# Single vector steps, one-pass turning and longer sums in a kernel that mixes a Fourier layer with sliding-window attention

## The chip, the cores and the metric

The kernel runs on one core of a Trainium2 chip. The engines named below are TensorE (PE in the rows of the profile, with its weight loads as PEld), VectorE (DVE), ScalarE (ACT), GpSimd (POOL) and SyncE (SP), which only issues DMAs here. The metric is the time of one execution in microseconds of the device; the time of a kernel is the median of its runs.

## The reference

x is 2048x512, float32. Two branches and a gate, with 32 heads of 16 and a window of 256:

```python
g = _sigmoid((x * gate_w).sum(-1, keepdims=True))
# A: Fourier mixing with matrices, hidden axis, then sequence axis, real part
a = jnp.einsum("bsd,ed->bse", x, dft_hid_re)
b = jnp.einsum("bsd,ed->bse", x, dft_hid_im)
y = jnp.einsum("ts,bse->bte", dft_seq_re, a) - jnp.einsum("ts,bse->bte", dft_seq_im, b)
# B: causal attention in a sliding window, then the output projection
scores = jnp.einsum("bhqd,bhkd->bhqk", q, k) * (Dh ** -0.5)
mask = (idx[:, None] - idx[None, :] >= 0) & (idx[:, None] - idx[None, :] < W)
p = _softmax(jnp.where(mask[None, None], scores, -1e9), axis=-1)
o = jnp.einsum("bhqk,bhkd->bhqd", p, v)      # then @ wo
out = g * y + (1 - g) * o
```

## The kernel before

**Dense products.** A float32 matrix product is made of three products in float32r, a type that TensorE takes in one pass: each operand is split into `hi` (the operand rounded to float32r, a CAST) and `lo` (operand less `hi`, a TENSOR_TENSOR), and hi·hi, hi·lo and lo·hi are summed in PSUM (`TERMS`). Tiles `dqk`, `dv`, `dab` and `dc` are the PSUM targets of the projections of q and k, of v, of the hidden Fourier step and of the sequence Fourier step. All of it is one generator, `dense()`, which yields after each 128x512 product. The matrices of the sequence step come in 64 pieces of 128x1024 (`c_pieces`, `load_split`): DMA into `raw`, two CASTs and two TENSOR_TENSORs of 512 columns on DVE into `hi` and `lo`, then 24 products.

**Attention.** There are 4 groups of 8 heads (`NG`) and 32 blocks of 64 positions (`NB`), so N = 128 blocks, each with 4 pairs of heads (`NP`). The loop runs over n:

- `s_pair(n, p)` (S): one product of up to 128x320 scores into PSUM (`s`), then on DVE a masked minimum, which reads `s` and frees it (line 327), then on ACT an exponential that yields the row sum (line 330). Minimum and sum of each query land in a column of `ml`.
- `ml_rows(u)`, once per 8 blocks: turns `ml` (128x64) into rows with a product by the float32 identity `ident` on TensorE (line 337), the result in a PSUM tile of the `s` ring; DVE takes it apart into `mhl` and `lt`; DMAs write them to DRAM. `m_ring(u)` reads the minima back into rows 96 to 99 of `ring[0]`.
- `t_pair(k, p)` (T), `LAG` = 20 blocks behind S: the transposed scores with the minimum taken off by those rows, into PSUM (`t`); ACT's exponential writes them into `pt` (line 389); POOL zeroes the corners outside the window by affine selects (lines 394 and 398).
- `pv(n)`: sums of `pt` times v in float32 into `o`, the four pairs side by side on 32 columns each (line 415), for three blocks at a time. v is spread into `vpad` by POOL (`v_spread`). When 512 positions are done, DVE multiplies by the reciprocals of the sums (loaded from DRAM at that moment, line 422) and the result goes to `o_scr`.
- `make_pad`: DVE (3) and ACT (1) copy a block of q or k into the stationary tiles `pads`.

The tiles `s` and `t` share a ring of four PSUM banks (`ps_a`).

**Order.** TensorE's order is written out by hand: in each half of a pair `fill(n)` draws products from `dense()` at a rate of `FILL_FIRST`, `FILL_PROJ` or `FILL_SEQ` per two halves (12, 14 and 14.4 products per block). The orders of the other engines come from a scheduler, except that `behind(...)` and `late(...)` keep an instruction behind the last marked one of an engine. After the last sum the rest of `dense()` follows, with the output projection (`wo_block`, line 669) ahead of each of the last blocks of the sequence step; `attention_done` loads and splits `wo` into the place of `ring[0]`.

```python
            if p == 2 and k % 3 == 0:
                for j in range(k - 3, k):
                    if 0 <= j < N:
                        pv(j)
                if maxima < 16 and n > 8 * maxima + 8:
                    ml_rows(maxima)
```

Of the kernel before, what the change touches and what calls it, by code (L numbers as in the profile page):

```python
# [25 lines left out]
LAG = 20  # L26
WARM = 8
SWITCH = 4
FILL_FIRST, FILL_PROJ, FILL_SEQ = 3.0, 3.5, 3.6
# [3 lines left out]
def fnet_window_mix(ctx: ExitStack, tc: tile.TileContext, xT, x, wqk, wv, wr, wi, cr, ci, wo, gw, out):  # L33
# [69 lines left out]

    def load_split(src, act=False):
        return split_raw(load_raw(src), act)
# [51 lines left out]
    ident = const.tile([P, P], F32, name="ident")  # L157
    nc.gpsimd.memset(ident, 1.0)
    nc.gpsimd.affine_select(ident, ident, pattern=[[1, P]], compare_op=OP.is_equal, fill=0.0,
# [60 lines left out]

    def qk_evict(g, ss, i, ps):
        hl = ev.tile([P, 2, 512], F32R, name="hl", bufs=3)
        split_psum(hl[:, 0], hl[:, 1], ps, -SCALE if i == 0 else 1.0)
        ld(qk_scr[i][g][ss].rearrange("h x s -> x h s"), f(hl[:]))
# [12 lines left out]
    def qk_proj(g, ss, w):  # L237
        for i in range(2):
            ps = ps_d.tile([P, 512], F32, name="dqk", tag="d")
            n = 0  # L240
            for dk in range(DK):
                c = dk * 256 + i * 128
                for a, b in TERMS:
                    nc.tensor.matmul(ps, w[a][:, c:c + 128], XT[dk, ss][:, b],  # L244
                                     start=n == 0, stop=n == 11)
                    n += 1
                    if n < 12:
                        yield
# [11 lines left out]
    def row_proj(sb, w, ps):  # L260
        n = 0
        ss, c = divmod(sb, 4)
        for dk in range(DK):
            wh = [w[dk // 2][h][:, (dk % 2) * 512:(dk % 2) * 512 + 512] for h in range(2)]
            for a, b in TERMS:
                nc.tensor.matmul(ps, XT[dk, ss][:, a, c * 128:(c + 1) * 128], wh[b],  # L266
                                 start=n == 0, stop=n == 11)
                n += 1
                if n < 12:
# [15 lines left out]
    def ab_proj(i, sb, w, dst=None):  # L285
        ps = ps_d.tile([P, 512], F32, name="dab", tag="d")
        yield from row_proj(sb, w, ps)
        if dst is None:
            hl = ev.tile([P, 2, 512], F32R, name="hl", bufs=3)
# [23 lines left out]
    ML = {}  # L313

# [17 lines left out]

    def ml_rows(u):
        ml = ML.pop(u)
        nc.vector.reciprocal(ml[:, 1], ml[:, 1])
        pt = ps_a.tile([P, 512], F32, name="s", tag="st")
        nc.tensor.matmul(pt[:64, :P], ml.rearrange("p x c -> p (x c)"), ident, start=True, stop=True)  # L337
        hl = at.tile([32, 2, 2, 64], F32R, name="mhl", bufs=1)
        m = pt[:32, :P].rearrange("c (a r) -> c a r", a=2)
        nc.vector.tensor_scalar(hl[:, :, 0], m, -1.0, None, op0=OP.mult)  # L340
        nc.vector.scalar_tensor_tensor(hl[:, :, 1], m, -1.0, f(hl[:, :, 0]), op0=OP.mult, op1=OP.subtract)
        ld(m_scr[u].rearrange("x p (j r) -> (p j) x r", r=64), f(hl[:]).rearrange("c a h r -> c (a h) r"))
        lt = at.tile([64, P], F32, name="lt", bufs=1)
        nc.vector.tensor_copy(lt[32:64], pt[32:64, :P])
        for a in range(2):
            ls = l_scr[u]
            ld(bass.AP(tensor=ls.tensor, offset=ls.offset + a * 512, ap=[[1024, NP], [64, 8], [1, 64]]),
               lt[32:64, 64 * a:64 * a + 64])
# [8 lines left out]
    PT = {}  # L357

# [42 lines left out]
    def pv(n):  # L401
# [17 lines left out]
        if kb % 8 == 7:  # L419
            sb = kb // 8  # L420
            ps = OT.pop((g, sb))
            rl = ev.tile([P, 512], F32, name="ev")
            ls = l_scr[g * 4 + sb]
            ld(rl, bass.AP(tensor=ls.tensor, offset=ls.offset, ap=[[512, 2 * NP], [0, 16], [1, 512]]))
            nc.vector.tensor_mul(rl, ps, rl)
            ld(o_scr[sb][g], rl)


    def c_pieces(order):
        w, todo = {}, list(order)  # L430

        def get(k):
            for _ in range(2 if k not in w else 1):
                if todo:
                    cc, j = todo.pop(0)
                    w[cc, j] = load_split((cr, ci)[cc][j // 2, j % 2])
            return w.pop(k)
        return get
# [4 lines left out]
    def c_part(w, chunks, ab, ps, ends):  # L443
        for i in chunks:
            for a, b in TERMS:
                nc.tensor.matmul(ps, w[a][:, i % 8 * 128:i % 8 * 128 + 128], ab[SC[i]][:, b],  # L446
                                 start=i == ends[0] and a + b == 0, stop=i == ends[1] and a == 1)
                if i != chunks[-1] or a == 0:
# [37 lines left out]
    def dense():  # L486
# [7 lines left out]
        yield  # L494
        for ss in range(4):
            if ss:
                yield from qk_proj(0, ss, wq0)
            for c in range(4):
# [4 lines left out]
                if ss < 3:  # L503
                    if c in (1, 2):
                        late(split_x, ss + 1, (2 * c - 2, 2 * c - 1), ss == 0)
                        if ss < 2:
                            load_x(ss + 2, c - 1)
                elif c == 0:
                    raw = load_raw(wqk[1])
                    wraw = [load_raw(wi[0])]  # L510
                elif c == 2:
                    w = late(split_raw, raw)
        for g in range(1, NG):
            for ss in range(4):
                yield from qk_proj(g, ss, w)
                have.add(("qk", g, ss))
                if g == 1:
                    if ss == 0:
                        wraw.append(load_raw(wi[1]))
                    elif ss < 3:  # L520
                        if ss == 1:
                            ws = []
                        ws.append(late(split_raw, wraw[ss - 1]))
                        if ss == 1:
                            raw = load_raw(wqk[2])
                elif g == 2:
                    if ss == 0:
                        raw = load_raw(wqk[3])
                        wraw = [load_raw(wr[0])]
                    elif ss == 2:  # L530
                        nextw = late(split_raw, raw)
                        wraw.append(load_raw(wr[1]))
                elif ss in (0, 2):
                    if ss == 0:
                        ws = []
                    ws.append(late(split_raw, wraw[ss // 2]))
            if g == 1:
                for sb in range(16):
                    yield from ab_proj(1, sb, ws)
                    if sb == 1:  # L540
                        nextw = late(split_raw, raw)
            if g < 3:
                w = nextw
        ab = {}
        for sb in range(16):
# [3 lines left out]
            if sb < 10:  # L549
                if sb < 8:  # L550
                    gate_load(sb)
                if sb > 1:
                    late(gate, 2 * sb - 4)
                    late(gate, 2 * sb - 3)
# [7 lines left out]

# [235 lines left out]
```

## Time and profile before

| | |
|---|---|
| median of three runs | 869.66 us (869.17 to 870.4) |
| the profiled execution | 873.39 us |
| its span, first to last instruction | 871.3 us |
| mean granted TensorE clock | 0.998 |
| busy: PE, PEld, DVE, ACT, POOL | 860.5, 690.3, 611.3, 580.9, 384.6 us |
| HBM read and written | 106.69 and 50.07 MB |

PE's busy time counts each product from its start to its modelled end, so neighbours overlap: a 128x512 product lasts 395 ns in the rows, but the next one starts much sooner. What TensorE loses is therefore read from the distance between starts, and from the idle time of the weight loads (PEld) before an instruction, not from the busy share. S runs to 660 us of the span, T to 752 and the sums to 759, and after that only dense products and the output projection are left.

### The profile page before, as it was taken

The page shows a single profiled execution, that of the slowest core. Times are in us where ns is not written, and L with a number is a line of the kernel's source. Part 1 is how long each engine was busy: PE and PEld are TensorE (multiplying, and loading weights), DVE is VectorE, ACT ScalarE, POOL GpSimd, SP SyncE. Part 2 cuts the span into 40 slices and gives each one's busy share as a digit, 9 for nine tenths or more (in the row PEclk, how much of TensorE's full clock was granted, in tenths as well). Part 3 has the DMA queues.
Part 4 walks back from the last instruction along what each step waited for, and adds up shares of the span by engine and source line. Part 5 has one row for each costly group of instructions (what it writes and reads, how often), then busy time and mean ns, then how long its engine had stood idle before and what let it go on. Part 6 is the DMA issues. An engine that isn't in the chain of part 4 may idle for free.

```text
span 871.3 us, 17146 instructions
## 1 busy us (share of the span) xinstructions
PE 860.5 (99%) x5160; PEld 690.3 (79%) x5160; DVE 611.3 (70%) x1974; ACT 580.9 (67%) x1793; POOL 384.6 (44%) x1067
## 2 busy tenths in 40 slices
PE   8999999999999999999999999999999999999998
PEld 6888778787877778878788887878778787788886
DVE  4588987667878987878787777788876444564431
ACT  4388799888897987878788777877776454111110
POOL 9100054545444756656456566554546665200000
PEclk9999999999999999999999999999999999999999
DMA  6875796464749436644445354599944333485541
GB/s 229 266 226 155 248 262 197 153 214 158 241 158 289 130 105 225 172 130 135 134 131 170 105 163 133 156 349 256 329 148 159 123 118 114 130 263 192 189 145 48
DMA packets 93132, 157.87 MB, mean 181 GB/s; under 512 B 27120, under 2 KB 36080, under 8 KB 93040
## 3 DMA queue, kind: packets, MB, share of 16 engines
q1 hardware_dynamic: 92288, 155.61, 56.5%
q10 hardware_dynamic: 752, 1.18, 0.4%
q8 instruction: 40, 0.66, 0.3%
q14 instruction: 52, 0.43, 0.2%
HBM read 106.69 MB, written 50.07 MB: 180 GB/s over the span
## 4 chain that ended last, share of the span: by engine, by line
PE 92%; DVE 3%; DMA 2%; ACT 1%; issue 1%; SPq 0%; DVEq 0%; ACTq 0%
PE dc L446 40%; PE dab L266 9%; PE s L325 8%; PE o L415 8%; PE dqk L244 8%; PE t L388 8%; PE t L669 5%; PE dv L266 4%; DVE sm L327 1%; PE s L232 1%; DMA raw<-x 1%; ACT sm L330 1%; DMA ring<-qk_scr 1%; PE s L337 1%; DMA pt<-xT 0%
## 5 line engine op out<-in xcount | busy, mean ns | idle before, releaser
L446 PE MATMUL dc<-big,hi 128*128 128x512 f32 x1024 | 355.4, 395 | 0.0
L394 POOL TENSOR_SCALAR_AFFINE_SELECT pt<-pt 64x128 f32<-64x128 f32 x512 | 191.9, 375 | 276.4 <-ACT pt L389 261.2
L330 ACT ACTIVATE sm<-sm,ml 128x320 f32<-128x320 f32 (+4 forms) x512 | 277.3, 543 | 49.4 <-DVE ml L327 48.0
L327 DVE CUSTOM_DVE_ANT_0 sm<-s,mask 128x320 f32<-128x320 f32 (+4 forms) x512 | 230.7, 462 | 82.7 <-PE s L325 62.5
L389 ACT ACTIVATE pt<-t 128x320 f32<-128x320 f32 (+4 forms) x512 | 208.7, 412 | 89.8 <-PE t L388 86.2
L446 PEld LDWEIGHTS dc<-big,hi 128*128 128x128 f32 x1024 | 186.3, 188 | 32.6 <-issue 2.4
L446 PE MATMUL dc<-big,lo 128*128 128x512 f32 x512 | 201.6, 394 | 0.0
L398 POOL TENSOR_SCALAR_AFFINE_SELECT pt<-pt 64x128 f32<-64x128 f32 x448 | 161.9, 361 | 0.1
L325 PE MATMUL s<-ring,pad 128*128 128x320 f32 (+4 forms) x512 | 159.0, 310 | 0.9 <-DVE ml L327 0.5
L388 PE MATMUL t<-ring,pad 128*128 128x320 f32 (+4 forms) x512 | 155.1, 303 | 1.6 <-DVE ml L327 0.9
L310 DVE TENSOR_SCALAR pad<-ring,half 96x256 fp32r<-96x256 f32 x384 | 121.6, 358 | 24.2 <-PE t L388 22.0
L325 PEld LDWEIGHTS s<-ring,pad 128*128 128x128 f32 x512 | 96.0, 188 | 36.6 <-issue 7.4
L388 PEld LDWEIGHTS t<-ring,pad 128*128 128x128 f32 x512 | 96.1, 188 | 21.6 <-DVE ml L327 2.6
L446 PEld LDWEIGHTS dc<-big,lo 128*128 128x128 f32 x512 | 96.3, 188 | 10.6
L81 DVE TENSOR_TENSOR lo<-raw,hi 128x512 fp32r<-128x512 f32 x146 | 99.6, 712 | 1.4 <-PE dc L446 1.3
L330 ACT ACTIVATION_READ_ACCUMULATOR sm<-sm,ml 128x1 f32 x512 | 98.8, 193 | 0.0
L266 PE MATMUL dab<-hi,big 128*128 128x512 f32 x256 | 90.9, 396 | 0.0
L244 PE MATMUL dqk<-big,hi 128*128 128x512 f32 x240 | 86.7, 394 | 0.6 <-DVE hl L86 0.5
L80 DVE CAST hi<-raw 128x512 fp32r<-128x512 f32 x142 | 58.6, 453 | 38.3 <-PE dc L446 37.1
L415 PE MATMUL o<-pt,vpad 128*32 128x320 f32 (+4 forms) x1408 | 73.8, 351 | 0.0
L378 POOL COPY vpad<-vr 64x256 f32<-64x256 f32 x64 | 26.0, 405 | 91.1 <-DMA vr<-v_scr 72.0
L308 ACT ACTIVATE pad<-ring,half 96x256 fp32r<-96x256 f32 x128 | 64.1, 500 | 0.0
(82 smaller groups left out, 780.3 us busy)
## 6 DMA issues: line engine op xcount, KB each, us to landing
qk_scr<-hl SPq DMA_DIRECT2D x32, 512.0 KB
ring<-qk_scr SPq DMA_DIRECT2D x32, 512.0 KB
raw<-cr SPq DMA_DIRECT2D x32, 512.0 KB
raw<-ci SPq DMA_DIRECT2D x32, 512.0 KB
ab_scr<-hl SPq DMA_DIRECT2D x20, 512.0 KB
big<-ab_scr SPq DMA_DIRECT2D x20, 512.0 KB
r_scr<-ev SPq DMA_DIRECT2D x36, 256.0 KB
ev<-r_scr SPq DMA_DIRECT2D x36, 256.0 KB
```

What stands on the lines that cost most here:

```text
L244: nc.tensor.matmul(ps, w[a][:, c:c + 128], XT[dk, ss][:, b], start=n == 0, stop=n == 11)
L266: nc.tensor.matmul(ps, XT[dk, ss][:, a, c * 128:(c + 1) * 128], wh[b], start=n == 0, stop=n == 11)
L310: nc.vector.tensor_scalar(dst, src, half[:96, h:h + 1], None, op0=OP.mult)
L325: nc.tensor.matmul(ps[:, :w], PAD[0, n][:, p], ring[1][:, p, k0:k0 + w], start=True, stop=True)
L327: mark("dve", nc.vector.tensor_tensor_reduce(out=sm[:, :w], in0=ps[:, :w], in1=mask[:, WIN - w:], scale=1.0, scalar=3e38, op0=OP.add, op1= ...
L330: mark("act", nc.scalar.activation(sm[:, :w], sm[:, :w], AF.Exp, bias=nm[:, c], scale=-1.0, accum_out=l[:, c]))
L388: nc.tensor.matmul(ps[:, :w], PAD[1, n][:, p], ring[0][:, p, q0:q0 + w], start=True, stop=True)
L389: nc.scalar.activation(pt[:, p, :w], ps[:, :w], AF.Exp, scale=-1.0)
L394: nc.gpsimd.affine_select(a, a, pattern=[[0, 2], [1, 64]], compare_op=OP.is_ge, fill=0.0, base=0, channel_multiplier=-1)
L398: nc.gpsimd.affine_select(a, a, pattern=[[0, 2], [-1, 64]], compare_op=OP.is_gt, fill=0.0, base=0, channel_multiplier=1)
L415: nc.tensor.matmul(OT[g, sb][32 * p:32 * p + 32, q - sb * 512:e - sb * 512], v2[:, p], pt[:, p, q - q0:e - q0], start=first, stop=kb == 8 ...
L446: nc.tensor.matmul(ps, w[a][:, i % 8 * 128:i % 8 * 128 + 128], ab[SC[i]][:, b], start=i == ends[0] and a + b == 0, stop=i == ends[1] and a ...
```

## The change

- **Single steps.** `split_soon` puts the two CASTs and two TENSOR_TENSORs of a split into a list `jobs`; `job(n)` takes one from it at every sixth dense product (n % 6 == 3). The splits of x, of the projections' weights and of the pieces, and the products of the gate (`gate_soon`), go through it. Pieces are loaded two ahead instead of one (`Pieces`), and each `get` first empties the list.
- **One-pass turning.** `ident` becomes float32r. `ml_split` (at block 8u+8) takes the reciprocals and splits `ml` into float32r `hi` and `lo`; `ml_turn` (8u+9, third pair) makes two products; `ml_rows` (8u+9, fourth pair) takes the rows out, adding hi and lo of the sums; `m_ring` comes at 8u+11.
- **Sums.** `pv` runs for three blocks at a time as long as projections last, then for five. For that `pt` has six places: four as before, and two in `home`, which until then holds the pairs on their way to `qk_scr` and `ab_scr` (before: tiles `hl` of another pool, three of them). v is loaded and spread when its place is free. The reciprocals of the sums are loaded ahead (`l_load`) and the multiplication stands in `o_out`, a block's start later.
- **Numbers.** `LAG` 20 to 18, `FILL_PROJ` 3.5 to 4.0 and `FILL_SEQ` 3.6 to 3.7, so 12, 16 and 14.8 products per block. The float32 sums stand in 31 groups instead of 43 on TensorE, and 231 instead of 322 dense products are left at the last T, 63 of them instead of 92 between the last sum and the first output block; that one then has 5, 6 and 5 blocks of output rows at a time instead of 4, 4, 4 and 4.

```diff
-LAG = 20
+LAG = 18
-FILL_FIRST, FILL_PROJ, FILL_SEQ = 3.0, 3.5, 3.6
+FILL_FIRST, FILL_PROJ, FILL_SEQ = 3.0, 4.0, 3.7
...
+    jobs = []
+
+    def split_soon(raw):
+        hi = st.tile([P, 1024], F32R, name="hi")
+        lo = st.tile([P, 1024], F32R, name="lo")
+        for c in HALVES:
+            jobs.append(lambda c=c: late(nc.vector.tensor_copy, hi[:, c], raw[:, c]))
+            jobs.append(lambda c=c: late(nc.vector.tensor_sub, lo[:, c], raw[:, c], f(hi[:, c])))
+        return hi, lo
+
+    def job(n):
+        if n % 6 == 3 and jobs:
+            jobs.pop(0)()
...
+    def ml_split(u):
+        ml = ML.pop(u).rearrange("p x c -> p (x c)")
+        MH[u] = at.tile([P, 2, NP * 16], F32R, name="mlh", bufs=1)
+        with behind("dve"):
+            nc.vector.reciprocal(ml[:, 32:], ml[:, 32:])
+            nc.vector.tensor_copy(MH[u][:, 0], ml)
+            mark("dve", nc.vector.tensor_sub(MH[u][:, 1], ml, f(MH[u][:, 0])))
+
+    def ml_turn(u):
+        hl = MH.pop(u)
+        MT[u] = ps_a.tile([P, 512], F32, name="s", tag="st")
+        for h in range(2):
+            nc.tensor.matmul(MT[u][:64, h * P:h * P + P], hl[:, h], ident, start=True, stop=True)
+
     def ml_rows(u):
-        ml = ML.pop(u)
-        nc.vector.reciprocal(ml[:, 1], ml[:, 1])
-        pt = ps_a.tile([P, 512], F32, name="s", tag="st")
-        nc.tensor.matmul(pt[:64, :P], ml.rearrange("p x c -> p (x c)"), ident, start=True, stop=True)
...
+        with behind("dve"):
+            nc.vector.tensor_scalar(hl.rearrange("c a h r -> c h a r"), m, -1.0, None, op0=OP.mult)
+            nc.vector.tensor_copy(lt, pt[32:64, :P])
+            mark("dve", nc.vector.tensor_add(lt, pt[32:64, P:2 * P], lt))
...
-            PT[n] = at.tile([P, NP, WIN], F32, name="pt", bufs=4)
+            if "proj" in have:
+                more.append(n)
+            c = (n - more[0]) % 6 * NP * WIN if more else 3072
+            if c + NP * WIN <= 3072:
+                PT[n] = f(home[:, c:c + NP * WIN].rearrange("p (a b) -> p a b", a=NP))
+            else:
+                PT[n] = at.tile([P, NP, WIN], F32, name="pt", bufs=4)
...
+    TURN = (8, 1, ml_split), (9, 2, ml_turn), (9, 3, ml_rows), (11, 3, m_ring)
...
+            if p == 3 and k % 8 == 6 and 0 <= k < N:
+                l_load(k // 8)
+            if p == 0 and full:
+                o_out()
+            if p == 2 and (k - summed >= (5 if more else 3) or k == N):
+                for j in range(summed, k):
+                    pv(j)
+                summed = k
```

How this moves the instructions, at the places of which the prediction speaks. First VectorE in the sequence step, between the masked minima of S (`ISA sm`), before:

```order
L327 ISA sm,ml<-s,mask 128x320
L327 ISA ml 128x1
L80 CAST hi<-raw 128x512 x2
L327 ISA sm,ml<-s,mask 128x320
L327 ISA ml 128x1
L81 TENSOR_TENSOR lo<-raw,hi 128x512 x2
L327 ISA sm,ml<-s,mask 128x320
L327 ISA ml 128x1
L425 TENSOR_TENSOR ev<-o,ev 128x512
```

The same engine at the same stage, now:

```order
L352 ISA ml 128x1
L546 TENSOR_TENSOR lo<-raw,hi 128x512
L352 ISA sm,ml<-s,mask 128x320
L352 ISA ml 128x1
L546 CAST hi<-raw 128x512
L352 ISA sm,ml<-s,mask 128x320
L352 ISA ml 128x1
```

Between two minima stood two CASTs or two TENSOR_TENSORs, and now one of them. Next TensorE at a group of sums that has a turning of `ml` behind it, before (`o<-pt,vpad` are the sums, `s<-ident,ml` the turning in float32):

```order
L446 MATMUL dc<-big,hi 128x512
L415 MATMUL o<-pt,vpad_327 32x256 x4
L415 MATMUL o<-pt,vpad_327 32x192 x4
L415 MATMUL o<-pt,vpad_327 32x128 x4
L337 MATMUL s<-ident,ml 64x128
L325 MATMUL s<-ring_268,pad_1_264 128x320
```

TensorE now, a group of sums in the same stage:

```order
L512 MATMUL dc<-big,hi 128x512
L460 MATMUL o<-pt,vpad_326 32x320 x4
L460 MATMUL o<-home,vpad_326 32x320 x8
L460 MATMUL o<-pt,vpad_326 32x320 x4
L460 MATMUL o<-pt,vpad_327 32x256 x4
L350 MATMUL s<-ring_268,pad_1_264 128x320
```

And TensorE now at a turning:

```order
L433 MATMUL t<-ring_267,pad_1_266 128x320
L512 MATMUL dc<-big,hi 128x512
L370 MATMUL s<-ident,mlh 64x128 x2
L350 MATMUL s<-ring_268,pad_1_264 128x320
L512 MATMUL dc<-big,lo 128x512
```

A group holds five blocks instead of three, and the turning stands alone between dense products and S.

More of the change, by code (lines that the diff above doesn't have):

```diff
@@ L494, in dense, with x_job @@
         yield
+        def x_job(ss, dk):
+            late(split_x, ss, (dk,), ss == 1)
+            if dk % 2 and ss < 3:
+                load_x(ss + 1, dk // 2)
         for ss in range(4):
+            if ss < 3:
+                for dk in range(DK):
+                    jobs.append(lambda ss=ss, dk=dk: x_job(ss + 1, dk))
+                    jobs.append(lambda: None)
             if ss:
                 yield from qk_proj(0, ss, wq0)
+            if ss == 3:
+                w = split_soon(raw)
             for c in range(4):
@@ L548, in dense @@
             yield from ab_proj(0, sb, ws, ab.get(sb))
[L549 to L554, printed above, removed]
+            if sb in (1, 3):
+                gate_load(6 + sb // 2)
+            if sb < 7:
+                gate_soon(9 + sb)
+            if sb in (5, 7):
+                pieces.load()
+            if sb == 11:
+                pieces.split()
         for sc in range(4):
@@ L710, in fnet_window_mix, with v_next @@
     need(("v", 5))
-    for n in range(N + LAG + 2):
+    summed, spread, fresh = 0, 2, 0
+    def v_next(n):
+        if n < N:
+            for c in range(2):
+                need(("v", n % NB // 2 + c))
+            with behind(*(("sp",) if n < 8 else ())):
+                v_load(n)
+    for n in range(N + LAG + 1):
         if n in (1, 3, 5):
```

183 lines of the change are left out of this document (104 added, 79 removed).

## The prediction

> **What bounds the kernel now.** I read the page's busy line and chain first, then the waits, then the timeline at single places.
>
> ```profile
> PE 860.5 (99%) x5160; PEld 690.3 (79%) x5160; DVE 611.3 (70%) x1974; ACT 580.9 (67%) x1793; POOL 384.6 (44%) x1067
> ...
> PE 92%; DVE 3%; DMA 2%; ACT 1%; issue 1%; SPq 0%; DVEq 0%; ACTq 0%
> ```
>
> The chain in order of time has the price of a product where nothing disturbs it (start, us, what):
>
> ```profile
> 812.82 10.88 PE dc L446 x48
> ```
>
> That is 10.88/48 = 0.227 us for 128x512. TensorE holds 92% of the chain that ended last; every other engine has room on the whole. So the time is TensorE's stream of products, plus what it loses between them. A change that adds nothing to that stream can only gain what is lost, or lose more. The losses that other engines cause are in the waits (waiting line, releaser: total us, times, longest):
>
> ```profile
> DVE mhl L340 <- PE s L337: 24.8, 16, 2.7
> ...
> PEld s L325 <- ACT sm L330: 3.6, 7, 0.5
> ...
> PEld s L325 <- DVE ml L327: 3.3, 9, 0.6
> ...
> PEld t L388 <- DVE ml L327: 2.6, 6, 0.8
> ...
> PEld s L325 <- ACT pt L389: 2.0, 4, 0.8
> PEld o L415 <- POOL pt L398: 1.6, 5, 0.4
> PEld s L325 <- DVE ev L425: 1.6, 3, 0.5
> ...
> PEld t L388 <- ACT pt L389: 1.5, 4, 0.6
> ...
> PEld dqk L244 <- DVE hl L88: 1.0, 2, 0.5
> ...
> PEld dqk L244 <- DVE hl L86: 0.9, 1, 0.9
> ```
>
> VectorE releases 9 + 6 + 3 + 2 + 1 = 21 of these waits, 3.3 + 2.6 + 1.6 + 1.0 + 0.9 = 9.4 us of the weight loader. How much of such a wait the products lose, and where it comes from, one place shows:
>
> ```profile
> 610.83 0.67 DVE L81 TENSOR_TENSOR lo<-raw,hi 128x512 fp32r<-128x512 f32 x1
> ...
> 611.43 0.46 DVE L310 TENSOR_SCALAR pad<-ring,half 96x256 fp32r<-96x256 f32 x1
> ...
> 611.81 0.77 DVE L81 TENSOR_TENSOR lo<-raw,hi 128x512 fp32r<-128x512 f32 x1
> ...
> 612.40 0.39 PE L446 MATMUL dc<-big,hi 128*128 128x512 f32 x1
> 612.50 0.48 DVE L327 CUSTOM_DVE_ANT_0 sm<-s,mask 128x320 f32<-128x320 f32 x1
> ...
> 613.04 0.19 PEld L325 LDWEIGHTS s<-ring,pad 128*128 128x128 f32 x1 [0.60 <-DVE ml L327]
> 613.04 0.41 PE L325 MATMUL s<-ring,pad 128*128 128x320 f32 x1 [0.26 <-DVE ml L327]
> ```
>
> Two steps of a split and a pad stand on VectorE ahead of the minimum that empties a bank of S; the next S needs the bank. From start to start it is 613.04 - 612.40 = 0.64 us here, and 0.23 for such a product undisturbed, so 0.41 is lost where the loader idled 0.60: idle time less 0.19. The 21 waits on VectorE are thus worth 9.4 - 21 x 0.19 = 5.4 us, and the 15 on ScalarE's lines 330 and 389 worth 7.1 - 15 x 0.19 = 4.2 us.
>
> **The change part by part.** *Groups of sums.* A float32 group costs TensorE more than its columns, at both edges:
>
> ```profile
> 354.33 0.31 PE L388 MATMUL t<-ring,pad 128*128 128x320 f32 x1
> 354.47 0.39 PE L446 MATMUL dc<-big,hi 128*128 128x512 f32 x1
> 354.80 1.84 PE L415 MATMUL o<-pt,vpad 128*32 128x192 f32 x48
> 356.56 0.42 PE L325 MATMUL s<-ring,pad 128*128 128x320 f32 x1
> 356.82 0.40 PE L446 MATMUL dc<-big,hi 128*128 128x512 f32 x1
> ```
>
> The dense product ahead of it takes 354.80 - 354.47 = 0.33 us instead of 0.23, and the S behind it 356.82 - 356.56 = 0.26, where the T above takes 354.47 - 354.33 = 0.14. That is 0.22 us a group, and the order has 12 groups fewer (31, not 43): 12 x 0.22 = **2.6 us off**. What a group costs inside beside its columns (1.76 us for three blocks) these rows don't part; I count nothing for it, as the columns stay the same.
>
> *Turning.* Before, one float32 turning of two passes; now two products in one pass each.
>
> ```profile
> 332.82 0.19 PE L325 MATMUL s<-ring,pad 128*128 128x64 f32 x1
> 332.85 0.48 PE L446 MATMUL dc<-big,hi 128*128 128x512 f32 x1
> 333.16 0.31 PE L388 MATMUL t<-ring,pad 128*128 128x320 f32 x1
> ...
> 341.09 0.43 PE L337 MATMUL s<-ident,ml 128*64 128x128 f32 x2
> 341.45 0.33 PE L325 MATMUL s<-ring,pad 128*128 128x128 f32 x1
> ```
>
> The old one takes 341.45 - 341.09 = 0.36 us. The new form is not in the trace; its nearest row is a float32r product with few columns. S of 64 columns and the dense product after it take 333.16 - 332.82 = 0.34 together, 0.11 over the dense product alone: the columns are short, but the next weights come no sooner. At 0.06 each (128 columns at 0.23/512) the pair would cost 0.11, at 0.11 each 0.22. I take 0.20, near the row, as the second load has only the first short product to hide in: 16 x (0.36 - 0.20) = **2.6 us off**, with 2.2 and 4.0 as ends. By the Trainium skill's page "TensorE: Matmul & The Clock Gate", section "LDWEIGHTS (loading the stationary operand)", a load takes its columns over 1.2 GHz, an estimate of 53 ns for these 64 columns; by that the pair would cost about 0.11 us and this term be 4.0 us.
>
> *Single steps.* The numbers of splits and gate products stay; their places change.
>
> ```profile
> L310 DVE TENSOR_SCALAR pad<-ring,half 96x256 fp32r<-96x256 f32 x384 | 121.6, 358 | 24.2 <-PE t L388 22.0 <-DMA ring<-qk_scr 1.0 <-PE s L325 0.7
> L81 DVE TENSOR_TENSOR lo<-raw,hi 128x512 fp32r<-128x512 f32 x146 | 99.6, 712 | 1.4 <-PE dc L446 1.3
> ...
> L80 DVE CAST hi<-raw 128x512 fp32r<-128x512 f32 x142 | 58.6, 453 | 38.3 <-PE dc L446 37.1 <-DMA raw<-ci 1.0
> ...
> L344 DVE COPY lt<-s 32x128 f32<-32x128 f32 x16 | 4.5, 283 | 0.5
> ```
>
> Two TENSOR_TENSORs between two minima are 2 x 0.712 = 1.42 us, with the three pads 2.5; one of them with the pads is 1.79. I added these means up over VectorE's whole order: work of over 2 us between two minima stands at 31 places before and 11 now, and what exceeds 2 us falls from 17.5 to 2.9 us. The turning adds two small steps per 8 blocks (of some 0.3 us each, like L344), which VectorE's free 30% covers; and the multiplication by -1 for the rows no longer stands right behind a group of sums, where VectorE waited 24.8 us for the turning (first row of the waits). Waits don't vanish in proportion, as pads and evictions still fall together: I take two thirds of the 5.4, **3.6 us off**; the ends are 0 and 5.4.
>
> *Numbers.* More dense products per block (16 and 14.8, not 14 and 14.4) leave fewer for the end (231, not 322); their sum is the same, so TensorE's stream is the same length. Each pair of S and T gets up to 0.5 x 0.23 = 0.11 us longer, which gives ScalarE and VectorE more time per block. I count nothing for it; the 4.2 us of waits on ScalarE might shrink by half. `LAG` 18 starts T two blocks sooner and costs no product. If minima came back too late for T, T would wait, but they are read at block 8u+11 and first used at 8u+14. *Loads ahead* of pieces and reciprocals lift waits that TensorE does not feel (VectorE waits for a piece's DMA only 1.0 us in all, row L80): nothing.
>
> **The sum.** 2.6 + 2.6 + 3.6 = 8.8 us. The profiled execution took 873.39 us, its span 871.3 and 2.1 around it, so it would take 864.6. The median of the runs shown, 869.66, lies 3.7 below the profiled execution; I take the gain off there: 869.66 - 8.8 = **860.9 us**.
>
> **The rivals.** *The first output block comes too early (R1).* The order leaves 63 dense products, not 92, between the last sum and the first output block.
>
> ```profile
> 758.30 0.54 PE L415 MATMUL o<-pt,vpad 128*32 128x128 f32 x16
> ...
> 769.21 0.62 ACT L78 CAST os<-ev 128x512 fp32r<-128x512 f32 x1 [16.80 <-DMA ev<-o_scr]
> 769.86 0.69 DVE L81 TENSOR_TENSOR os<-ev,os 128x512 fp32r<-128x512 f32 x1 [3.85 <-ACT os L78]
> ```
>
> From the end of the last sum (758.84) to its first block split (770.55) it took 11.7 us, through VectorE, two DMAs and ScalarE. The cover is now 63 x 10.88/48 = 14.3 us. It holds by 2.6; SP's queue has a piece's load ahead of that read, which waits for the split of `wo`'s second half. If that puts 3 to 6 us on the way, TensorE waits up to 3.4: 864.3. Chance 0.14.
>
> *The waits stay (R2).* Steps now fall between nearly all minima; if each wait avoided is paid for at another place, the edges and turnings alone remain: 869.66 - 5.2 = 864.5, and with as many new waits on the turning's bank, held by VectorE's third step, as are saved (5.2), 869.7, no change. Chance 0.10.
>
> *Slower: selects held up by splits (R3).*
>
> ```profile
> 610.45 1.30 POOL L394 TENSOR_SCALAR_AFFINE_SELECT pt<-pt 64x128 f32<-64x128 f32 x1
> ...
> 612.69 0.29 POOL L398 TENSOR_SCALAR_AFFINE_SELECT pt<-pt 64x128 f32<-64x128 f32 x1
> ```
>
> A select that meets VectorE's split (610.83, above) shows 1.30 us, one that meets none 0.29: 1.0 more. With a split step in nearly every pair, the last select ahead of a group of sums meets one more often; were each of the 18 groups of five blocks held up for that 1.0 us, TensorE would lose 18 us: 860.9 + 18 = 879. It decides when POOL ends a block's selects over half a block after its T. Against it: POOL is busy 44% of the span, the group waits until the third pair of the next block, and the sums waited for line 398 five times for 1.6 us. The Trainium skill has the rule on the page "SBUF — State Buffer", section "SBUF: two separate sides": VectorE's steps with two SBUF inputs and GpSimd share a pair of ports as an exclusive lock, and whoever starts second is blocked for the whole instruction; the 1.30 agrees. Chance 0.07.
>
> *All waits go (R4)*, on VectorE (5.4) and half on ScalarE (2.1), and the turning is cheap (4.0): 869.66 - 14.1 = 855.6. Chance 0.12.
>
> **How the numbers follow.** My forecast has 0.57, R1 0.14, R2 0.10, R3 0.07, R4 0.12. The range 855.5 to 868 holds the forecast with its terms' ends, R1, R4 and half of R2. A difference of 0.2%, 1.7 us, is about what a measurement of this kernel can tell from none: faster is all but R3 and part of R2, 0.86; same 0.06; slower 0.08.
>
> **What would show it.** In the new profile: 31 groups with the same 0.22 at the edges; two turning products at 0.2 us a pair; under 2 us of waits of PEld on lines of the minima; TensorE's first output product without idle time ahead of it. A wait of PEld on POOL of over 5 us would be R3, idle time ahead of the output projection R1. If the span falls by less than 4 us with all of that as forecast, losses between products that no wait shows have grown, and the account is wrong.

## The result and the profile after

The kernel after takes 870.33 us (median of 14 runs, 867.32 to 874.2), the kernel before beside it 870.31 us (14 runs, 869.17 to 874.53): ratio 0.9996, 95% interval 0.9981 to 1.0012. No change can be measured; the forecast was 860.9, with 855.5 to 868.0 as its range. The profiled execution of after took 868.91 us, its span 867.2.

Busy line and chain of the page of after:

```profile
PE 853.2 (98%) x5160; PEld 693.5 (80%) x5160; DVE 616.4 (71%) x2006; ACT 588.4 (68%) x1793; POOL 371.6 (43%) x1067
...
PE 94%; DMA 3%; DVE 1%; issue 0%; ACT 0%; ACTq 0%; POOL 0%; SPq 0%; DVEq 0%
```

TensorE is busy 7.3 us less than before (860.5), which is the direction that fewer group edges and a cheaper turning give, and yet the chain has DMAs for 3% (2% before), and 14.0 us of the span are idle on TensorE (10.8 before): it stands still more. The waits say where (waiting line, releaser: total us, times, longest):

```profile
PE s L350 <- ACT pt L434: 7.6, 2, 4.1
...
ACT pt L434 <- DMA big<-ab_scr: 4.8, 1, 4.8
ACT pt L434 <- DMA l_scr<-mhl: 4.3, 1, 4.3
PEld s L350 <- DVE ml L352: 3.6, 10, 0.6
...
DVE mhl L379 <- PE s L370: 2.6, 1, 2.6
```

VectorE's wait for the turning, 24.8 us before, is down to 2.6. The longest wait on a minimum is still 0.6. New are two long waits on ScalarE's exponential of T (line 434): 7.6 us of TensorE in two pauses, each of which ended when ScalarE had waited for a DMA. Stage by stage (window: us, busy time of the engines with counts, granted clock, DMA share, GB/s), before:

```profile
550.00:575.00 25.00, 25.00 (x186) 19.72 (x185) 17.79 (x63) 18.81 (x60) 13.25 (x38) 1.00 0.80 250
575.00:600.00 25.00, 24.80 (x137) 19.27 (x137) 22.58 (x80) 19.76 (x69) 10.22 (x28) 1.00 0.91 301
600.00:625.00 25.00, 24.74 (x158) 19.74 (x157) 21.20 (x69) 19.98 (x63) 14.02 (x40) 1.00 1.04 333
```

and after:

```profile
550.00:575.00 25.00, 22.92 (x155) 17.76 (x153) 19.74 (x68) 16.08 (x51) 11.76 (x37) 1.00 1.01 271
575.00:600.00 25.00, 22.88 (x149) 18.54 (x150) 17.23 (x56) 16.86 (x56) 10.07 (x26) 0.93 0.78 258
600.00:625.00 25.00, 21.39 (x138) 17.14 (x137) 19.61 (x69) 16.16 (x54) 10.01 (x27) 1.00 1.00 284
```

This is the stretch in which the sixteen 512 KB tiles of the second half of the sequence step are loaded (`next_b`, `big<-ab_scr`). In both kernels the DMA share reaches 1.0 there; only after stands still. The first pause in the timeline of after:

```profile
559.92 0.38 SPq L56 DMA_DIRECT2D big<-ab_scr  x1
...
561.40 0.52 SPq L56 DMA_DIRECT2D ring<-qk_scr  x1
564.05 0.32 SPq L56 DMA_DIRECT2D m_scr<-mhl  x1
564.48 0.57 SPq L56 DMA_DIRECT2D ring<-qk_scr  x1
565.10 0.58 SPq L56 DMA_DIRECT2D big<-ab_scr  x1
...
571.68 0.19 ACT L355 ACTIVATION_READ_ACCUMULATOR sm<-sm,ml 128x1 f32 x1
...
575.88 0.64 ACTq L391 DMA_DIRECT2D ring<-m_scr  x1
576.63 0.44 ACT L434 ACTIVATE pt<-t 128x320 f32<-128x320 f32 x1 [4.75 <-DMA big<-ab_scr]
...
577.12 0.42 PE L350 MATMUL s<-ring,pad 128*128 128x320 f32 x1 [4.07 <-ACT pt L434]
```

ScalarE is done at 571.87 and then stands at `m_ring`, the DMA that brings the rows of minima back from DRAM, which it issues at 575.88 only. Behind `m_ring` in its queue are the exponentials that empty the PSUM banks, so TensorE stops. `m_ring` waits for two things: for the store `m_scr<-mhl` (issued 564.05), and for its own DMA semaphore. The program gives its hardware DMAs eight semaphores in turn, and a DMA is issued when the transfer that had its semaphore before has landed; here that is a `big` load issued after the store, and it landed at 575.80. In order of time the chain shows that load from issue to landing (start, us), and for the second pause a store of sums in the same part:

```profile
565.10 10.70 DMA big<-ab_scr
...
613.61 9.15 DMA l_scr<-mhl
```

The landings by the trace's semaphore updates: the two stores of minima took 10.0 and 10.1 us (564.05 to 574.05, 610.03 to 620.16); before, the stores in that stretch took 5.7 and 3.8. Of ScalarE's 4.0 and 3.6 us at `m_ring`, the stores account for 2.2 and 0.9, the semaphores for 1.8 and 2.6.

After the pause there is a second price (windows as above):

```profile
577.00:578.00 1.00, 0.88 (x3) 0.78 (x4) 0.43 (x3) 1.00 (x5) 0.00 (x0) 0.79 0.99 375
578.00:580.00 2.00, 2.00 (x7) 1.66 (x6) 1.32 (x6) 1.34 (x5) 1.55 (x4) 0.50 0.81 249
580.00:582.00 2.00, 2.00 (x10) 1.68 (x9) 1.85 (x7) 1.38 (x4) 1.08 (x4) 0.75 0.88 327
```

The granted clock is 0.50 for 3.4 us, and a dense product takes 0.43 us from start to start instead of 0.23. Counted that way, the two pauses cost 4.2 and 3.7 us and the slow products behind them about 1.7 each, some 11 us in all (the expectation of the first run counts 10.5). A run below that has neither pause is 8.8 us faster than this kernel.

### The profile page after: what moved, and what is told of

It is laid out like the page before. It is cut to its first block, busy times and chain, and to the rows that moved or that the text cites. A ratio compares the mean times of both kernels' runs of the same rounds, so it can differ in the third digit from the quotient of the medians.

```text
span 867.2 us, 17211 instructions
## 1 busy us (share of the span) xinstructions
PE 853.2 (98%) x5160; PEld 693.5 (80%) x5160; DVE 616.4 (71%) x2006; ACT 588.4 (68%) x1793; POOL 371.6 (43%) x1067
## 4 chain that ended last, share of the span: by engine, by line
PE 94%; DMA 3%; DVE 1%; issue 0%; ACT 0%; ACTq 0%; POOL 0%; SPq 0%; DVEq 0%
PE dc L512 39%; PE dab L288 10%; PE dqk L265 9%; PE s L350 9%; PE o L460 8%; PE t L433 8%; PE dv L288 5%; PE t L754 5%; DMA big<-ab_scr 1%; DMA vr<-v_scr 1%; DMA l_scr<-mhl 1%; PE s L253 1%; PE dv L551 0%; DVE pad L333 0%; DVE sm L352 0%
## 5 line engine op out<-in xcount | busy, mean ns | idle before, releaser
L352 DVE CUSTOM_DVE_ANT_0 sm<-s,mask 128x320 f32<-128x320 f32 (+4 forms) x512 | 235.5, 464 | 117.7 <-PE s L350 91.5
L439 POOL TENSOR_SCALAR_AFFINE_SELECT pt<-pt 64x128 f32<-64x128 f32 x392 | 139.5, 356 | 228.5 <-ACT pt L434 217.3
L434 ACT ACTIVATE pt<-t 128x320 f32<-128x320 f32 (+4 forms) x392 | 160.5, 411 | 59.2 <-PE t L433 48.0
L433 PE MATMUL t<-ring,pad 128*128 128x320 f32 (+4 forms) x512 | 155.1, 303 | 0.1
L333 DVE TENSOR_SCALAR pad<-ring,half 96x256 fp32r<-96x256 f32 x384 | 119.3, 358 | 19.0 <-PE t L433 18.6
L350 PEld LDWEIGHTS s<-ring,pad 128*128 128x128 f32 x512 | 96.5, 188 | 42.3 <-ACT pt L434 10.5
L443 POOL TENSOR_SCALAR_AFFINE_SELECT pt<-pt 64x128 f32<-64x128 f32 x344 | 117.4, 341 | 0.0
L433 PEld LDWEIGHTS t<-ring,pad 128*128 128x128 f32 x512 | 96.7, 189 | 21.7 <-DVE ml L352 0.9
L546 DVE TENSOR_TENSOR lo<-raw,hi 128x512 fp32r<-128x512 f32 x142 | 97.7, 698 | 0.0
L288 PE MATMUL dab<-hi,big 128*128 128x512 f32 x256 | 89.1, 393 | 0.0
L265 PE MATMUL dqk<-big,hi 128*128 128x512 f32 x240 | 84.9, 393 | 0.0
L439 POOL TENSOR_SCALAR_AFFINE_SELECT home<-home 64x128 f32<-64x128 f32 x120 | 48.1, 401 | 61.2 <-ACT home L434 53.3
L546 DVE CAST hi<-raw 128x512 fp32r<-128x512 f32 x142 | 61.3, 443 | 16.2 <-PE dc L512 15.8
```

What stands on the lines that cost most here:

```text
L265: nc.tensor.matmul(ps, w[a][:, c:c + 128], XT[dk, ss][:, b], start=n == 0, stop=n == 11)
L333: nc.vector.tensor_scalar(dst, src, half[:96, h:h + 1], None, op0=OP.mult)
L350: nc.tensor.matmul(ps[:, :w], PAD[0, n][:, p], ring[1][:, p, k0:k0 + w], start=True, stop=True)
L352: mark("dve", nc.vector.tensor_tensor_reduce(out=sm[:, :w], in0=ps[:, :w], in1=mask[:, WIN - w:], scale=1.0, scalar=3e38, op0=OP.add, op1= ...
L433: nc.tensor.matmul(ps[:, :w], PAD[1, n][:, p], ring[0][:, p, q0:q0 + w], start=True, stop=True)
L434: nc.scalar.activation(pt[:, p, :w], ps[:, :w], AF.Exp, scale=-1.0)
```

## The experiments

**The theory (A):** ScalarE, in order, stands at `m_ring` while the DMAs are slow, and that eats the gain. **Rivals:** the rows are too late for T anyway (B); the gain was never there (C); only the semaphore's former user holds `m_ring`, not the store (D). The differences below are between medians. The kernel before, taken again beside each group of runs, stood at 870.05 to 870.86 us, and by the ratios to it some of these differences come out up to 1 us smaller. First, `m_ring` one block later in the order:

```diff
-    TURN = (8, 1, ml_split), (9, 2, ml_turn), (9, 3, ml_rows), (11, 3, m_ring)
+    TURN = (8, 1, ml_split), (9, 2, ml_turn), (9, 3, ml_rows), (12, 3, m_ring)
```

> The kernel after, with the transfer of the minima's rows to the ring (m_ring, issued by ScalarE) one block later: (12, 3) for (11, 3). Theory A (ScalarE stands in its queue at m_ring until the rows' store has landed, twice for about 4 us, and TensorE with it): both pauses of TensorE (4.2 and 3.7 us) and the slow products behind them go, 870.3 - 10.5 = 859.8 us (858 to 862), and no wait on ACT pt over 1.5 us is left. Rival B (the rows simply come too late while the DMAs are busy): T waits for the rows instead, twice 3 to 6 us on DMA ring, 868 to 873. Rival C (the pauses are not what eats the gain): they go, and the time stays above 866.

Measured 864.42 us (863.15 to 865.17), 0.9937 of before (0.9925 to 0.9949). One number in the order gives 5.9 us. The longest wait on ACT pt is 0.5, no T waits for its rows (against B), and the time fell below 866 (against C). It is not 859.8, because one dense product now waits for a `big` load in the same stretch:

```profile
PEld dc L512 <- DMA big<-ab_scr: 2.2, 1, 2.2
PEld s L350 <- ACT pt L434: 2.0, 4, 0.5
PE dc L512 <- DMA big<-ab_scr: 1.8, 1, 1.8
```

The other way round, `m_ring` three quarters of a block earlier, where by the program's waits it stands, in the first of the two places, for its store alone:

```diff
-    TURN = (8, 1, ml_split), (9, 2, ml_turn), (9, 3, ml_rows), (11, 3, m_ring)
+    TURN = (8, 1, ml_split), (9, 2, ml_turn), (9, 3, ml_rows), (11, 0, m_ring)
```

> The kernel after with m_ring three quarters of a block earlier, (11, 0) for (11, 3): ScalarE reaches it 4.4 us earlier. In the trace of after, by the semaphores, the two stores landed at 574.05 and 620.16, 2.2 and 0.9 us after ScalarE stood at m_ring, and the transfers that had m_ring's semaphore before it landed 1.75 and 2.6 us later still. At (11, 0) m_ring of block 12 waits for its store alone. Theory A (the store's landing): ScalarE stands there 6.6 and 5.3 us, TensorE loses as much more as ScalarE, 870.3 + 4.3 = 874.6 us (872 to 877). Rival D (the semaphore's former user alone holds m_ring): the pauses of blocks 12 and 13 go, about 860 to 863.

Measured 872.54 us (867.86 to 875.51), 1.0023 of before (1.0004 to 1.0041; after's own interval, 0.9981 to 1.0012, touches it). The chain has the store from issue to landing, the waits have ScalarE behind it:

```profile
565.09 10.06 DMA m_scr<-mhl
...
ACT pt L434 <- DMA m_scr<-mhl: 12.6, 2, 6.4
...
PE t L433 <- ACT pt L434: 5.2, 1, 5.2
PE s L350 <- ACT pt L434: 5.1, 1, 5.1
```

D falls: with no foreign semaphore in the way the pause is longer. ScalarE stood 5.7 and 5.5 us at `m_ring` (6.6 and 5.3 expected), TensorE 2.7 us more in the two pauses than in after, and the time rose by 2.2, not by 4.3.

Why does the store take 10 us? It was put on ScalarE's own DMA queue:

```diff
-        ld(m_scr[u].rearrange("x p (j r) -> (p j) x r", r=64), f(hl).rearrange("c a h r -> c (a h) r"))
+        MH[u] = hl
...
+    def m_store(u):
+        with behind("act"):
+            nc.scalar.dma_start(m_scr[u].rearrange("x p (j r) -> (p j) x r", r=64),
+                                f(MH.pop(u)).rearrange("c a h r -> c (a h) r"))
...
-    TURN = (8, 1, ml_split), (9, 2, ml_turn), (9, 3, ml_rows), (11, 3, m_ring)
+    TURN = (8, 1, ml_split), (9, 2, ml_turn), (9, 3, ml_rows), (10, 2, m_store), (11, 3, m_ring)
```

> The kernel after, with the store of the minima's rows to DRAM issued by ScalarE's queue (at (10, 2)) and not by SyncE's; m_ring stays at (11, 3). If the store is late because it stands behind the large loads in SyncE's DMA queue (queue theory), it now lands in under 7 us in the same stretch, ScalarE doesn't wait, and the time is 859 to 862. If it is late because all 16 DMA engines are busy, whichever queue it comes from (saturation theory), it takes over 10 us again, both pauses stay at 3 us or more, and the time is 867 to 872.

Measured 867.69 us (865.13 to 874.48), ratio 0.9985 (0.9968 to 1.0002). The trace is of the execution that took 874.48. By the semaphore updates the two stores took 8.6 and 7.9 us, less than 10 but far from the 1.5 to 5.6 us of this run's other stores, and both pauses stayed, at 3.3 and 2.8 us. That lies between the two expectations, nearer to the second:

```profile
580.40 0.44 ACT L439 ACTIVATE pt<-t 128x320 f32<-128x320 f32 x1 [4.09 <-DMA l_scr<-mhl]
580.89 0.63 PE L350 MATMUL s<-ring,pad 128*128 128x320 f32 x1 [3.32 <-ACT pt L439]
```

So the store is slow from another queue too. The Trainium skill gives a reason on the page "DMA: Bandwidth & Descriptors", section "Issuing engines are not separate DMA queues": DMAs from any engine run on the same 16 DMA engines and interleave there. The 8.6 and 7.9 us agree. The run does not show that another queue could never help: its stores were issued 5.6 us ahead of the moment at which ScalarE was ready for `m_ring`, in after 7.8 and 9.2.

What stands ahead of the store in after are loads of the ring (issued 561.40 above). `LAG` sets their place:

```diff
-LAG = 18
+LAG = 20
```

> The kernel after with LAG 20 for 18: loads of the ring are issued two blocks later, so that they stand behind the store of the minima's rows in SyncE's queue, not right ahead of it. Queue theory: the store lands in under 9 us, both pauses go, 859 to 863. If the sixteen 512 KB loads of the second half alone delay the store (theory of the switch), the pauses stay: 867 to 872.

Measured 866.49 us (865.09 to 874.0), ratio 0.997 (0.9953 to 0.9987). The trace is of the slowest execution, 874.0, so its pauses are larger than the median's. The SyncE rows now have the store ahead of the ring:

```profile
561.45 0.38 SPq L56 DMA_DIRECT2D m_scr<-mhl  x1
...
566.09 1.28 SPq L56 DMA_DIRECT2D ring<-qk_scr  x2
```

and the two stores landed in 3.9 and 2.8 us. That part of the theory holds: with `LAG` 18 the ring's loads stand ahead of these two stores, and that makes them late. But the time is not 859 to 863. `m_ring` waited 2.0 us for a ring load that had its semaphore, and VectorE met the same queue at another place, the addition of r:

```profile
617.55 14.72 DMA ev<-r_scr
...
DVE ev L663 <- DMA ev<-r_scr: 6.5, 1, 6.5
PE t L433 <- DVE ml L352: 5.2, 1, 5.2
```

A load that took 14.7 us held VectorE for 6.5 and TensorE for 5.2. With `LAG` 20 and `m_ring` two blocks later as well:

```diff
-LAG = 18
+LAG = 20
...
-    TURN = (8, 1, ml_split), (9, 2, ml_turn), (9, 3, ml_rows), (11, 3, m_ring)
+    TURN = (8, 1, ml_split), (9, 2, ml_turn), (9, 3, ml_rows), (13, 3, m_ring)
```

> The kernel after with LAG 20 and m_ring at (13, 3), as far ahead of its first T as before: the loads of the ring stand behind the stores, and ScalarE reaches m_ring two blocks later than in the LAG 20 run. If m_ring was the only place at which the queues of that stretch stop TensorE: no pause over 1.5 us, 861 to 863. If the stretch's delays of 10 to 15 us stop another engine that waits in order (in the LAG 20 run VectorE stood 6.5 us at the addition of r, and TensorE 5.4): one such pause stays, 864 to 868.

Measured 865.78 us, ratio 0.9947 (0.9927 to 0.9966): ScalarE never waits at `m_ring`, and the pause at VectorE's addition stays, at 3.6 us by the waits (`PE t L433 <- DVE ml L352`). The second expectation it is. The rates alone:

```diff
-FILL_FIRST, FILL_PROJ, FILL_SEQ = 3.0, 4.0, 3.7
+FILL_FIRST, FILL_PROJ, FILL_SEQ = 3.0, 3.5, 3.6
```

> The kernel after with the old rates (FILL_PROJ 3.5, FILL_SEQ 3.6): the sixteen loads of the second half move by about a block against the blocks of S, the loads of the ring stay right ahead of the store. Queue theory: at least one store still has loads of the ring and of the second half ahead of it, so at least one pause of 3 us or more stays: 864 to 870. If it was only the chance meeting of the two (coincidence theory), both pauses go: 859 to 863.

Measured 866.04 us (864.14 to 868.29), ratio 0.9959 (0.9945 to 0.9973): one store (583.17) took 11.6 us, ScalarE stood 2.3 us, one pause of 2.3 us stayed, less than the 3 expected, and the other was gone, since the first store now lies ahead of the heavy stretch (it landed in 1.5 us).

Then the loads of the second half, spread over twice as many half blocks:

```diff
-SWITCH = 4
+SWITCH = 8
...
-            if after:
+            if after and c == 0:
```

> The kernel after with m_ring where it is, but the sixteen 512 KB loads of the second half spread over twice as many half blocks (SWITCH 8, one load a half block, not SWITCH 4 and two). If the DMA engines' load in that stretch makes the store of the rows late (saturation theory, which the store on ScalarE's own queue spoke for), the DMA share falls from 1.05 to about 0.85, both pauses of TensorE fall under 1 us each, and the time is 860 to 864. Rival: the loads of the ring ahead of the store do it; then the pauses stay at 3 us or more, and the time is 867 to 872.

Measured **861.51 us** (858.66 to 863.68), 0.9906 of before (0.989 to 0.9921), the fastest of all and faster than both kernels. No pause is over 0.9 us (windows of this run):

```profile
550.00:575.00 25.00, 24.86 (x166) 19.83 (x165) 21.46 (x73) 18.96 (x62) 13.16 (x40) 1.00 0.95 272
...
600.00:625.00 25.00, 24.40 (x152) 19.78 (x151) 22.23 (x74) 19.82 (x64) 13.99 (x39) 1.00 0.94 278
```

The time is as expected, the reason less so: the DMA share fell to 0.95 over 25 us, not to 0.85, and the stores still took 8.8 and 10.0 us. They landed just before ScalarE needed them (571.84 for 572.02, 613.35 for 613.82), and no semaphore held `m_ring` there for more than 0.6. That is a narrow escape, not a cure. `SWITCH` 8 also sends eight more blocks of the sequence step through DRAM half done (45 stores of `r_scr`, not 37), so the spread is not all that it changes. With `m_ring` later as well:

> Both: m_ring one block later and the loads of the second half spread (SWITCH 8). The wait of 2.0 us of a dense product for such a load (and some 0.5 us of slow products behind it), which m_ring later alone left, goes as well: 864.4 - 2.5 = 861.9 us (861 to 864). If the load in that stretch cost nothing beyond the two pauses: 864.4, no change against m_ring later alone.

Measured 862.72 us (861.74 to 863.93), ratio 0.9912 (0.9898 to 0.9925): no pause over 1.1 us in that stretch. The wait for a `big` load is gone; against the run above there is no difference to be measured. The control, `SWITCH` 8 in the kernel before:

> Control: the kernel before, with the loads of the second half spread (SWITCH 8, one a half block). Before has no pause of TensorE over 1 us in that stretch; what it lost there above its other stages is about 1.7 us. If the spread helped the kernel after only by keeping ScalarE from being held at m_ring, before gains little: 868.5 to 870.5. If spreading is a gain of its own: 861 to 864, as the kernel after got from it.

Measured 870.01 us, ratio 0.9992 (0.9979 to 1.0006): spreading those loads is worth nothing where no engine is caught. What it took from after was the pauses.

**The sizes of the terms,** on the kernel with `m_ring` one block later (864.42). The steps again in bursts:

```diff
-        if n % 6 == 3 and jobs:
+        while n % 24 == 3 and jobs:
             jobs.pop(0)()
```

> m_ring one block later, and VectorE's splits and gate products again in bursts (all queued steps of a piece after its third product, not one after every sixth). It sizes the term of the single steps by itself, against 864.4. The prediction's term: 3.6 us slower, 868.0. By what the products lost to VectorE in the two traces (3.9 us before, 2.6 with m_ring later): 1.3 slower, 865.7. No use at all: 864.4.

Measured 869.35 us, ratio 0.9987 (0.9979 to 0.9996): 4.9 us slower (4.4 by the ratios). The waits:

```profile
PEld t L433 <- DVE ml L352: 3.4, 9, 0.9
PEld s L370 <- DVE mlh L364: 3.0, 2, 1.7
```

A new one is among them: the turning of after needs a split by VectorE ahead of it, and bursts hold that up at two places. From the first product of a pair to the next product, the 16 turnings take 5.5 us here and 2.5 without bursts. So about 3.0 of the 4.9 us are a cost that bursts would have only with the new turning. Groups of three throughout:

```diff
-            if p == 2 and (k - summed >= (5 if more else 3) or k == N):
+            if p == 2 and (k - summed >= 3 or k == N):
```

> m_ring one block later, and groups of sums of three blocks throughout, not five late. It sizes the term of the groups, against 864.4. The prediction's term: 12 groups more by 0.22 us, 2.6 slower, 867.0. By the traces (all groups and the product ahead of them took 75.1 us before and 72.1 with m_ring later): 3.0 slower, 867.4. If longer groups hold up S and T as much as they save: 864.4.

Measured 868.71 us, ratio 0.9977 (0.9968 to 0.9986): 4.3 slower (3.5 by the ratios). Added up over the two traces, less what the products ahead cost undisturbed, the 43 groups with the products ahead of them take 75.1 us and the 31 take 72.4; the products behind them lose 1.3 us more. In this trace the one long wait for a `big` load is also longer, 3.0 us and with slow products behind it. The old turning, with `ident` and `ml` in float32:

```diff
-        for h in range(2):
-            nc.tensor.matmul(MT[u][:64, h * P:h * P + P], hl[:, h], ident, start=True, stop=True)
+        nc.tensor.matmul(MT[u][:64, :P], ml, ident, start=True, stop=True)
```

> m_ring one block later, and the old turning: one float32 product of two passes on the unsplit minima and sums, placed as in after. It sizes the term of the turning, against 864.4. The prediction's term: 16 x 0.16 = 2.6 us slower, 867.0. By the traces (the turning took 0.36 us before and 0.154 a pair with m_ring later): 3.3 slower, 867.7. If the turning's time is hidden in the waits around it: 864.4.

Measured 864.64 us, ratio 0.9938 (0.9919 to 0.9958): 0.2 slower, with some 2 us of uncertainty from the two intervals. On TensorE the old form does cost what it cost before, 0.36 us; the profiled span is 1.5 us longer (863.2 and 861.7). The term is smaller than its price on TensorE. The waits show a part of the rest: with `m_ring` one block later the weight loader waits 13 times, 5.4 us, for VectorE's minima ahead of S and T, and 12 of these waits stand within 7 us behind a turning; with the old form it waits there 4 times, 2.5 us, one of them behind a turning, and 6 times, 2.1 us, ahead of the turning itself. So the new turning costs waits behind it that the old one does not. Whether the bank that it keeps or VectorE's additional steps cause them was not tested.

## Why the prediction was wrong

**The step that failed** stands under *Numbers*: "`LAG` 18 starts T two blocks sooner and costs no product. If minima came back too late for T, T would wait, but they are read at block 8u+11 and first used at 8u+14." It asked when T needs the rows, and not who stands in line behind the read. The read is an instruction in ScalarE's queue, and it waits there for a store. I counted nothing for it; it cost about 11 us in the trace, and 5.9 us came back when it was moved one block. `LAG` 18 was not free either: it put the ring's loads ahead of the two stores (10.0 and 10.1 us, against 3.9 and 2.8 with 20). The two blocks between store and read looked like before's; what I did not look at was how long a DMA takes in the stretch in which its share is 1.0, and what is issued ahead of the store there.

**Loads ahead: nothing.** The prediction looked at waits of before that would go, not at ones to come. What the loads ahead add to the full DMA engines in that stretch was not tested.

**Groups of sums: 2.6.** The edges were right, the term rather small. The edges of a group of five in after:

```profile
370.39 0.40 PE L512 MATMUL dc<-big,lo 128*128 128x512 f32 x1
370.72 0.75 PE L460 MATMUL o<-home,vpad 128*32 128x128 f32 x16
...
373.56 0.41 PE L350 MATMUL s<-ring,pad 128*128 128x320 f32 x1
373.81 0.62 PE L512 MATMUL dc<-big,hi 128*128 128x512 f32 x2
```

The dense product ahead of it takes 0.33 us and the S behind it 0.25, about as before. The run with 12 groups more lost 2.7 us in the groups and ahead of them and 1.3 behind, so a group also costs something inside, for which the prediction counted nothing.

**Turning: 2.6, ends 2.2 and 4.0.** The price on TensorE was too high, the worth too high as well:

```profile
391.72 0.39 PE L512 MATMUL dc<-big,hi 128*128 128x512 f32 x1
391.95 0.28 PE L370 MATMUL s<-ident,mlh 128*64 128x128 f32 x2
392.07 0.36 PE L350 MATMUL s<-ring,pad 128*128 128x320 f32 x1
```

The pair takes 392.07 - 391.95 = 0.12 us here, and 0.152 in the mean of the 16, not 0.20: the row that I took as nearest, a short product whose next weights come late, was the wrong one, and the 0.11 that the prediction worked out from the Trainium skill (page "TensorE: Matmul & The Clock Gate", section "LDWEIGHTS (loading the stationary operand)") was near. By the 0.152 the term is 16 x 0.21 = 3.4, yet undoing it moved the time by 0.2, in part because of the waits that the new form brings.

**Single steps: 3.6, ends 0 and 5.4.** 4.9 when undone, inside the ends, but not as argued: the waits on minima fell only from 3.3 + 2.6 to 3.6 + 0.9 us, where I had named under 2 us as the sign. Their places say more than their sum. Of the 15 in before one stands within 7 us behind a turning, of the 13 in after 12 do: the waits of the splits are nearly gone, and those behind the new turning came. Of the 4.9, some 3.0 are bursts holding up the new turning, a worth that the prediction did not have.

**The sum.** Where nothing is caught, the change comes near to what was forecast: 861.5 us (`SWITCH` 8) and 862.7 (with `m_ring` later too) against 860.9. That the sum is so near is in part luck. The three terms undone one by one are 4.9 + 4.3 + 0.2 = 9.4, near the 8.8 of the sum, but in other shares, and on a kernel that is only 5.9 faster than after; they don't add up, as bursts meet the new turning and the groups the long waits of that stretch.

**The rivals.** R1 did not come: the output projection waits for nothing (line 754: idle 0.0). R3 did not: sums waited for GpSimd 1.5 us in all. By the record the select of 1.30 us, on which R3's price rests, started 0.38 us ahead of the split that it met, so that row does not show which of the two held the other up. R2, 864.5 to 869.7, came in part: the 12 waits behind turnings in after are new. They hold the weight loader for 4.0 us, which by the prediction's own count (idle time less 0.19 each) loses about 1.8 us, not the 5.2 that its 869.7 needs; that this figure is near the measured time is luck. None had the way of the minima through DRAM, which is what decided. The last sign of the prediction's list, a span that falls by less than 4 us with all else as forecast, was not the case either: the span fell by 4.1 us, and the losses are in the waits, under ScalarE.

**Profile and median.** The 3.7 us between the profiled execution of before and its median were rightly left out. Most of them lie at the start: in its first 25 us (window 0 to 25) before's execution shows

```profile
0.00:25.00 25.00, 21.27 (x77) 16.53 (x78) 12.15 (x19) 11.58 (x21) 23.55 (x42) 0.93 0.62 213
```

and after's shows

```profile
0.00:25.00 25.00, 23.47 (x90) 18.74 (x91) 12.96 (x25) 12.18 (x22) 23.55 (x41) 1.00 0.79 259
```

These are 13 products fewer, some 3 us: in before's, TensorE stood 2.0 us at 5.3 and then ran at half clock for 3.4 us. Of the profiled executions of the experiments, `SWITCH` 8 with `m_ring` later started late in the same way (77 products), the store on ScalarE's queue later still (73), and most of the others did not, so this belongs to the execution and not to a kernel.

## What to carry to other kernels

When an instruction moves, ask of the queue it stands in: what does it wait for there, and what stands behind it; a DMA issued by a computing engine that waits for another DMA stops that engine and everyone whose buffers it frees. Price such a wait with the slowest stretch of the program, not with its mean: the store that landed within 2 to 8 us in the other stages took 10 where the DMA share was 1.0. And look at what the program puts ahead of a small urgent transfer, and at the semaphores that transfers share.

## What the hardware showed that was not expected

The granted clock falls after pauses as short as 2.0 us, but not after each. The page "TensorE: Matmul & The Clock Gate" of the Trainium skill, section "Part 1: The HAM clock gate (the "warmup" mystery)", gives an idle window of about 3.4 us for that. The pauses of 4.1 and 3.6 us would agree, but in the `LAG` 20 run TensorE sat idle 2.04 us ahead of the product that started at 577.60, and the windows then show:

```profile
577.50:578.50 1.00, 0.90 (x3) 0.77 (x4) 0.45 (x3) 1.00 (x5) 0.00 (x0) 0.78 0.92 293
578.50:581.50 3.00, 3.00 (x10) 2.50 (x9) 1.64 (x8) 2.15 (x8) 1.28 (x4) 0.51 0.99 362
```

In the run with the old turning a longer pause left the clock at 1.00:

```profile
622.65 0.72 PE L509 MATMUL dc<-big,hi 128*128 128x512 f32 x2 [2.29 <-DMA big<-ab_scr]
...
622.70:624.00 1.30, 1.30 (x7) 1.13 (x8) 0.45 (x1) 0.44 (x1) 0.79 (x2) 1.00 0.91 343
```

What parts the two is where the pause lies. By the clock records of the 14 traces, the clock changes only at points that are a whole number of 3.41 us apart within a run (in after at 577.58, 580.99, 625.36 and 628.78). Cut each run into pieces along these points, and add up TensorE's idle time in each piece. Up to the last product, every piece with 1.96 us of it or more has a piece at 0.50 behind it; a piece at full clock with 1.92 or less never has. The 2.04 us lie in one piece, the 2.29 are cut into 1.7 and 0.6. So in these traces no single pause length decides. Each fall cost about 1.7 us (after's two and the `LAG` 20 run's at 578.05) on top of the pause.
